# Permuted q, k and v rows, two-bank score tiles, a token MLP per pair, and transposes moved from TensorE to DMA in an attention + mixer kernel

## The chip, the core and the metric

The kernel runs on one core of one Trainium2 chip. The metric is device microseconds (us) of one execution. The four executions of the kernel before spread over 0.5% (465.88 to 467.99 us). The engines are named as in the profile: PE is TensorE's matmuls, PEld its weight loads (they overlap PE: in the kernel before 415.4 and 250.1 us of a span of 463.9), DVE is VectorE, ACT is ScalarE, POOL is GpSimd, SP is SyncE, which here only issues DMAs. PEclk is the clock that TensorE was granted, as a share of full speed. A run is called fast when it is at most 1.5% above the fastest of the same kernel beside it, else slow.

## The reference, cut to what matters

```python
# q, k, v: 8 batches x 12 heads x 448 rows x 64, float32
q_n = q / (norm(q) + 1e-6);  k_n = k / (norm(k) + 1e-6)
attn = softmax(q_n @ k_n.T / tau)            # 448 x 448 for each head
x = (attn @ v).transpose(0, 2, 1, 3).reshape(8, 448, 768)
h = relu(x.T @ w_tok1) @ w_tok2              # token MLP, 448 -> 256 -> 448
u = x + h.T
out = u + relu(u @ w_ch1) @ w_ch2            # channel MLP, 768 -> 1536 -> 768
```

Two heads are handled together as a *pair*: there are 48 pairs, numbered 0 to 47, six for each batch. q, k and v are loaded by the *half batch*, six heads or three pairs at a time: 672 KB each for q, k and v.

## The kernel before

For each pair GpSimd and VectorE normalise q and k; TensorE transposes them (eight 112x112 transposes); TensorE computes scores; ScalarE takes the exponential; TensorE multiplies with v ("PV"). While the pairs of batch b run, TensorE's free slots are filled with the MLPs of the batches before. Three parts matter here. First, a pair's scores use a single PSUM tile of four banks, so a score must wait for the exp before it:

```python
    ps2 = ctx.enter_context(tc.tile_pool(name="ps2", bufs=1, ...))
    def score(i, cg):                      # called twice a pair
        psS = ps2.tile([128, 2, 2, 512], FP32, ...)
        for j in range(2):
            for hh in range(2):
                nc.tensor.matmul(psS[:, hh, j, 0:S], ...)
        nc.scalar.activation(out=st["pt"][:, cg], in_=psS[0:SC, :, :, 0:S], func=AF.Exp, scale=inv_tau)
```

Second, q/k are transposed on TensorE, and VectorE copies the result out of PSUM:

```python
    def tpose(i):
        for a, src in enumerate((st["kn"], st["qn"])):
            for c in range(NCH):
                nc.tensor.transpose(pst[:, a, c, :], src[:, c], id16[:SC, :SC])
        nc.vector.tensor_copy(out=qk[:], in_=pst[:].rearrange("p a c s -> p a (c s)"))
```

Third, the residuals are added on TensorE by matmuls with an identity (four in token layer two, three in each output tile):

```python
        for i in range(3):
            nc.tensor.matmul(psF[:, 128 * i:128 * (i + 1)], rows(ut, 3 * dh + i), id16[:], start=False, stop=(i == 2))
        ...                                # [cut: VectorE / ScalarE copies to SBUF, stores]
```

## Time and profile before

| | before |
|---|---|
| median of 4 runs (465.88 to 467.99) | 467.04 us |
| span of the profiled run, mean granted clock | 463.9 us, 0.997 |
| PE busy | 415.4 us, 90% |
| bytes moved by DMA | 50.02 MB |
| eighth pair's (pair 7's) first score | 67.55 us |

From the page of the kernel before: the busy time of each engine, PE's busy tenths in 40 equal slices with the granted clock below them, and the chain of work that ended last, by engine.

```profile
PE 415.4 (90%) x4136; PEld 250.1 (54%) x4136; DVE 218.9 (47%) x442; ACT 232.1 (50%) x262; POOL 218.8 (47%) x220
...
PE   0505889999999999999999999999999999999995
...
PEclk9999999999999999999999999999999999999998
...
PE 84%; ACT 6%; DVE 4%; POOL 2%; issue 2%; DMA 1%; SPq 0%; ACTq 0%; POOLq 0%
```

PE is the bound: 90% busy, 84% of the chain. The page has its granted clock at 9 tenths or more in all slices but the last. No other engine is over half busy. So work taken off TensorE should shorten the run, as long as TensorE keeps its inputs.

From the timeline of the kernel before, around 33, 67 and 202 us (start, duration, engine, line, what; in brackets the idle time before it and what ended it):

```profile
33.81 0.93 PE L199 MATMUL psS_1_290<-qk_185 64*128 64x448 f16 x4 [10.95 <-ACT pt_251 L201]
...
67.55 0.56 PE L199 MATMUL psS_0_714<-qk_666 64*128 64x448 f16 x4 [1.14 <-ACT pt_630 L201]
...
201.68 0.55 PE L199 MATMUL psS_0_2815<-qk_2767 64*128 64x448 f16 x4 [1.14 <-ACT pt_2723 L201]
```

In the start, scores take 0.93 us for four matmuls and wait for others, once 11 us. Later they take 0.55, and now and then wait up to 1.14 us for the exp that still holds the only score tile.

### The profile page before, as it was taken

What the parts mean: (1) busy time and instruction counts of PE and PEld (TensorE: products, weight loads), DVE (VectorE), ACT (ScalarE), POOL (GpSimd) and SP (SyncE); (2) the same over time, 40 slices, a digit from 0 to 9 for tenths busy, and PEclk for the clock granted to TensorE, in tenths of its full rate; (3) what the DMA queues carried; (4) which work ended last, traced back from release to release, by engine and by line L of the source; (5) the groups of instructions that cost most, each with busy time, mean ns of one, the idle gap of its engine ahead of it and who ended that gap; (6) DMA issues with size and microseconds to landing.
All of it is one profiled execution on the core that took longest, in us unless ns stands there. A gap on an engine that the chain in (4) does not pass through costs nothing.

```text
span 463.9 us, 9519 instructions
## 1 busy us (share of the span) xinstructions
PE 415.4 (90%) x4136; PEld 250.1 (54%) x4136; DVE 218.9 (47%) x442; ACT 232.1 (50%) x262; POOL 218.8 (47%) x220
## 2 busy tenths in 40 slices
PE   0505889999999999999999999999999999999995
PEld 0203556556654566555655566556655666556563
DVE  2558659555564455445645445445735343224000
ACT  2324666775467544574457443674367534520410
POOL 4699698678374834374383725474472200000000
PEclk9999999999999999999999999999999999999998
DMA  9997999951485046721574065902100001000012
GB/s 205 237 235 175 223 204 229 209 120 32 125 188 119 1 129 154 167 47 37 134 192 102 1 165 117 206 9 78 52 35 1 35 35 56 15 34 35 34 54 83
DMA packets 72842, 50.02 MB, mean 108 GB/s; under 512 B 44449, under 2 KB 68449, under 8 KB 72801
## 3 DMA queue, kind: packets, MB, share of 16 engines
q1 hardware_dynamic: 69408, 44.05, 39.6%
q0 software_dynamic: 3392, 5.37, 6.3%
q8 instruction: 32, 0.52, 0.5%
q14 instruction: 10, 0.07, 0.1%
HBM read 43.78 MB, written 11.01 MB: 118 GB/s over the span
## 4 chain that ended last, share of the span: by engine, by line
PE 84%; ACT 6%; DVE 4%; POOL 2%; issue 2%; DMA 1%; SPq 0%; ACTq 0%; POOLq 0%
DMA qh_105<-in_q_dram 1%; DVE kn_324 L175 1%; DVE ssq_118 L157 1%; ACT pt_630 L201 1%; ACT pt_482 L201 1%; ACT pt_1042 L201 1%; DVE ssq_126 L157 0%; POOL sq_207 L152 0%; PE psF_2_1_5429 L279 0%; PE psF_2_0_5377 L279 0%; PE psF_1_1_5303 L279 0%; PE psF_0_0_5164 L279 0%; PE psF_2_1_4787 L279 0%; PE psF_2_0_4717 L279 0%; PE psF_1_1_4651 L279 0%
## 5 line engine op out<-in xcount | busy, mean ns | idle before, releaser
L260 PEld LDWEIGHTS <-wc1t 128*128 128x128 f16 x576 | 51.5, 97 | 52.0 <-issue 10.7
L279 PEld LDWEIGHTS <-gt_2_3862 128*128 128x128 f16 x168 | 15.3, 98 | 12.8 <-issue 2.6
L279 PEld LDWEIGHTS <-gt_1_2351 128*128 128x128 f16 x168 | 15.4, 98 | 12.5 <-issue 2.6
L279 PEld LDWEIGHTS <-gt_0_804 128*128 128x128 f16 x168 | 15.5, 98 | 11.4 <-issue 1.5
L279 PEld LDWEIGHTS <-gt_3_5342 128*128 128x128 f16 x168 | 15.9, 98 | 9.6
L228 PEld LDWEIGHTS <-w1t 128*128 128x128 f16 x128 | 10.9, 97 | 8.0 <-issue 2.6
L199 PE MATMUL psS_1_290<-qk_185 64*128 64x448 f16 x4 | 0.9, 557 | 11.0 <-ACT pt_251 L201 11.0
L183 PE MATMUL pst_145<-id_86,kn_143 112*128 112x112 f16 x4 | 0.6, 291 | 9.1 <-DVE kn_143 L175 9.1
L199 PEld LDWEIGHTS <-qk_185 64*128 64x128 f16 x8 | 0.5, 104 | 13.6 <-issue 12.9
L285 DVE COPY ost_0_6031<-psF_0_0_6032 128x384 f32<-128x384 f32 x1 | 0.6, 557 | 15.2 <-PE psF_0_0_6032 L282 15.2
L164 ACT ACTIVATE rn_119<-ssq_118,tiny 112x16 f32<-112x16 f32 x3 | 0.9, 307 | 12.1 <-DVE ssq_118 L157 12.1
L175 POOL TENSOR_TENSOR qn_5044<-qh_4311,rn_4315 112x512 f16<-112x512 f32 x1 | 1.0, 1041 | 10.3 <-DVE rn_4315 L167 10.3
L164 ACT ACTIVATE rn_109<-ssq_108,tiny 112x16 f32<-112x16 f32 x3 | 0.9, 304 | 8.6 <-DVE ssq_108 L157 8.6
L183 PEld LDWEIGHTS <-kn_143 112*128 112x128 f16 x4 | 0.3, 129 | 9.1 <-DVE kn_143 L175 9.1
L175 DVE TENSOR_TENSOR kn_324<-kh_116,rn_119 112x512 f16<-112x512 f32 x1 | 4.7, 4745 | 0.0
L282 PEld LDWEIGHTS <-ut_0_803 128*128 128x128 f16 x42 | 3.5, 98 | 1.8
L282 PEld LDWEIGHTS <-ut_1_2350 128*128 128x128 f16 x42 | 3.5, 98 | 1.8
L282 PEld LDWEIGHTS <-ut_2_3861 128*128 128x128 f16 x42 | 3.5, 98 | 1.8
L282 PEld LDWEIGHTS <-ut_3_5341 128*128 128x128 f16 x42 | 3.5, 98 | 1.8
L175 POOL TENSOR_TENSOR qn_3954<-qh_3191,rn_3195 112x512 f16<-112x512 f32 x1 | 1.0, 1042 | 7.3 <-PE psU_3_3986 L252 7.3
L199 PE MATMUL psS_0_400<-qk_365 64*128 64x448 f16 x4 | 0.9, 564 | 3.8 <-DVE qk_365 L185 3.8
L152 POOL TENSOR_TENSOR sq_2301<-qh_2033 112x512 f32<-112x512 f32 x1 | 1.0, 1039 | 6.9 <-DVE ssq_1701 L157 6.9
(1726 smaller groups left out, 1299.7 us busy)
## 6 DMA issues: line engine op xcount, KB each, us to landing
wc1t<-in_moe_w_ch_dram POOLq DMA_DIRECT2D x2, 1152.0 KB, 13.0
wc2t<-in_moe_w_ch_dram POOLq DMA_DIRECT2D x2, 1152.0 KB, 15.4
vs_107<-in_v_dram SPq DMA_DIRECT2D x1, 672.0 KB, 7.8
qh_115<-in_q_dram SPq DMA_DIRECT2D x1, 672.0 KB, 10.2
kh_116<-in_k_dram SPq DMA_DIRECT2D x1, 672.0 KB, 12.2
vs_117<-in_v_dram SPq DMA_DIRECT2D x1, 672.0 KB, 8.3
qh_123<-in_q_dram SPq DMA_DIRECT2D x1, 672.0 KB, 10.8
kh_124<-in_k_dram SPq DMA_DIRECT2D x1, 672.0 KB, 12.6
```

What stands on the lines that cost most here:

```text
L152: nc.gpsimd.tensor_mul(out=sq[:, a], in0=src, in1=src)
L157: nc.vector.tensor_reduce(out=half[i // HP]["ssq"][:, :, lo:lo + 2 * NCH], in_=pipe[i]["sq"][:], axis=AXX.X, op=ALU.add)
L164: nc.scalar.activation(out=rn, in_=ssq, func=AF.Ln, bias=tiny[:])
L175: eng.tensor_tensor(out=dst[:].rearrange("p c g e -> p g c e"), in0=src, in1=_bcast_free(rn, E), op=ALU.mult)
L183: nc.tensor.transpose(pst[:, a, c, :], src[:, c], id16[:SC, :SC])
L199: nc.tensor.matmul(psS[:, hh, j, 0:S], qk[hb:hb + 64, c * SC:c * SC + 128], qk[hb:hb + 64, S:2 * S], start=True, stop=True)
L201: nc.scalar.activation(out=st["pt"][:, cg], in_=psS[0:SC, :, :, 0:S], func=AF.Exp, scale=inv_tau)
L228: nc.tensor.matmul(psR[:], w1t[:, m, tt * 128:(tt + 1) * 128], x16[b][:, m, dh * DH:(dh + 1) * DH], start=(m == 0), stop=(m == 3))
L260: nc.tensor.matmul(psG[:], wc1t[:, dt, ct * 128:(ct + 1) * 128], ut[:, dt, span(b)], start=(dt == 0), stop=(dt == DT - 1))
L279: nc.tensor.matmul(psF[:], rows(gt, ct), wc2t[:, ct, dh * DH:(dh + 1) * DH], start=(ct == 0), stop=False)
L282: nc.tensor.matmul(psF[:, 128 * i:128 * (i + 1)], rows(ut, 3 * dh + i), id16[:], start=False, stop=(i == 2))
L285: nc.vector.tensor_copy(out=o[:, 0:DH], in_=psF[:])
```

## The change

The intent is to take about 27 us off TensorE and to fill the start. q's rows are permuted as k's and v's already were (row `4p + c` in place of `112c + p`), so each partition reads 1 KB runs of all three, and the token MLP's weights and the output's rows follow that order. The score tile becomes two tiles of two banks. The token MLP runs for each pair by itself, which gives u by rows; VectorE adds both residuals. u of pairs 6 to 47, and q/k of pairs 12 to 47, are transposed by DMA (`DMA_TRANSPOSE`) on SP's queue, where the q, k, v loads and the output stores are issued too. The diff, cut to its core:

```diff
-    outp = ctx.enter_context(tc.tile_pool(name="outp", bufs=3))
-    ps2 = ...(tc.tile_pool(name="ps2", bufs=1, space=bass.MemoryType.PSUM))
+    outp = ctx.enter_context(tc.tile_pool(name="outp", bufs=2))
+    ps2 = ...(tc.tile_pool(name="ps2", bufs=2, space=bass.MemoryType.PSUM))
+    DMA_T0 = 12
...
+    def tpose_dma(i):
+        st["qk"] = att.tile([128, 2, NCH, SC], FP16, name=f"qk_{i}", tag="qk")
+        nc.sync.dma_start_transpose(out=st["qk"][:]..., in_=st["kq"][:]...)
...
+    def tok2(i, pe=False):
+        ...                                        # eight 128x128 matmuls into psU
+        nc.vector.tensor_tensor(out=u, in0=psU[:], in1=st["x"][:], op=ALU.add)
+        if pe: return
+        nc.sync.dma_start_transpose(out=ut[b][:, pj], in_=u.rearrange("p m d -> p (m d)"))
...
-        for i in range(3):
-            nc.tensor.matmul(psF[:, 128 * i:128 * (i + 1)], rows(ut, 3 * dh + i), id16[:], ...)
+            nc.vector.tensor_tensor(out=o..., in0=psF..., in1=u16[bb]..., op=ALU.add)
...
+            # in the loop over pairs, pairs 0 to 5:
+                done = [[], [], [], [0, 1], [2, 3], [4]][i]
+                for t in done:
+                    tok1(t)
+                    tok2(t, pe=True)
+                    upose(t)
+            # pairs 6 and on:
+            if i % HP == 1 and (i + 8) // HP < NHALF:
+                load_half((i + 8) // HP)           # q, k and v, 2 MB, every third pair
+            if DMA_T0 <= i + 1 < NP_ALL:
+                tpose_dma(i + 1)                   # for the next pair
+            ...                                    # [cut: scores, PV, MLP pieces of pair i]
```

## The prediction

> **What bounds the kernel now.** TensorE. On the page PE is busy 90% of the 463.9 us span; the chain that ended last is 84% PE. From the timeline I took each matmul group's slot (start to next start, unstalled): score 4 matmuls 0.48 us, PV 16 in 0.51, four transposes 0.20 (8 and a gap: 0.49), token layer one 4x384 0.65, token layer two 0.37 plus its four identity matmuls 0.19, channel layer one 6x448 1.13, channel layer two 12x384 1.95 plus three identity matmuls 0.16. Times their counts this is 388 us. The rest: 9 us before the first matmul, 38 us of stalls and slow early matmuls up to 60 us (pair 7's score starts at 67.5 us), 23 us of later stalls (mostly score waiting for exp to free its single 4-bank tile, 1.14 us each), 5 us after the last matmul.

> **TensorE work removed and added.** Transposes of pairs 12-47: -36x8 at 0.05 = -14.4 us. Output identity matmuls: -8.8. Token layer two with identities 26.9 -> 48x8x0.056 = 21.5 (-5.4). Token layer one 20.8 -> 21.5 (+0.7). PE transposes of u, six pairs: +1.3. Sum -26.6: 388 -> 362 us. All on the critical path.

> **Start.** The stretches show DMA saturated until about 92 us at 205-215 GB/s while 256 B q rows load, 250-300 when only 1 KB runs do. Permuted q has 1 KB runs; ACT and POOL norm work is reordered, which held exp of pair 1 until 32 us (waits: ACT on ssq_118, on POOL sq_207). Exp becomes 4x about 0.93 instead of 2x1.66 us a pair (estimate). Six pairs at about 5.5 us (POOL, ACT and DVE each 4-5 us) from about 10 us, also doing five pairs' token MLP: pair 7 starts at about 47 us instead of 67.5. wc1t must land by then: 11 MB at 250 GB/s = 44 us, tight.

> **After that.** 362 less 23 us done by then = 339 us of PE slots. Two score tiles remove most 1.14 us waits; 8 us stalls stay. DVE gains adds but loses copies; ACT loses 13.4 us of output copies, gains about 19 us of exp overhead; both stay under 70%.

> **DMA transposes.** 36 of 229 KB, 42 of 131 KB, on SP's queue. None is in this trace. [...]against one pair (7.4 us) of lead. But every third pair three 672 KB loads are queued directly ahead (k lands 1.9 us after q): the transpose lands about 10 us after issue and score waits 1-3 us, ten times or so. Output stores with two buffers also queue behind loads. Together 12 us.

> **Sum.** 47 + 339 + 8 + 12 + 5 = 411; tuning may hide part: **408 us, 80% range 394 to 428**. Faster by over 2%: 0.96, same 0.03, slower 0.01.

> **What would show it.** Slots as above; pair 7's score start near 47 us; no score waits on ACT over 1 us in steady state; waits of score on DMA qk in every third pair; final 5 us unchanged.

> **What would make it wrong.** DMA transposes far slower than copies (over 7 us each stalls every pair: 450 or more); small token matmuls limited by weight loads; wc1t late; DVE blocked by output buffers; or transposes entirely hidden and a start under 42 us (near 393).

The sum: 47 + 339 + 8 + 12 + 5 = 411, and 3 less for tuning, 408. The landing of about 10 us behind three loads fits the prediction's own 205 to 215 GB/s: three loads of 672 KB are 2.06 MB, which is 9.6 to 10.1 us at that rate.

## The result, and the profile after

Ratios here and below are the mean time of one kernel's fast runs over that of the other's fast runs of the same rounds, so not quite the ratio of the medians that are quoted.

| | before | after |
|---|---|---|
| median | 467.04 us | 522.53 us (518.23 to 525.93, 4 runs) |
| ratio, 95% interval | | 1.1186 (1.1123 to 1.1249): slower |
| span, mean granted clock | 463.9, 0.997 | 522.0, 0.902 |
| PE busy | 415.4 us (90%) | 416.1 us (80%) |
| bytes moved by DMA | 50.02 MB | 63.87 MB |
| pair 7's first score | 67.55 us | 75.66 us |

The result is correct. The predicted 408 us was far off, and on the wrong side.

The same lines of the page, after (and the chain by line):

```profile
PE 416.1 (80%) x4056; PEld 249.7 (48%) x4056; DVE 208.0 (40%) x436; ACT 233.8 (45%) x362; POOL 213.9 (41%) x222
...
PE   1575687969695897949879496984949999999996
...
PEclk9995689898988797988979699896988999999999
...
PE 63%; DMA 20%; POOL 7%; issue 4%; DVE 3%; ACT 2%; SPq 0%; DVEq 0%; POOLq 0%
PE psG L324 20%; PE psF L339 19%; DMA qk<-kq 19%; PE psO L275 10%; PE psS L259 8%; POOL sq L199 3%; PE psU L302 3%; PE psR L288 3%; POOL kq L230 3%; DMA kh<-in_k_dram 1%; DVE ssq L208 1%; ACT pt L261 1%; POOL vt L184 1%; PE pst L244 0%; DVE ost L343 0%
```

Three things are to be seen. PE's row, all 9s before, has a dip to 4 or so at regular distances, until about 400 us. The granted clock has dips at the same places. And the transposes of q/k by DMA are now 19% of the chain. PE's busy time did not fall (416.1 us against 415.4), although it has less work (4056 matmuls against 4136): it does it more slowly, at a mean granted clock of 0.902 against 0.997.

The waits of PE's scores after (total us, times, longest):

```profile
PE psS L259 <- DMA qk<-kq: 62.5, 10, 9.3
...
PE psS L259 <- ACT pt L261: 3.3, 5, 1.5
```

Ten waits, 62.5 us. The waits for the exp, which the two-bank tiles were to remove, are indeed nearly gone. One of the ten, from the timeline of the kernel after, with what SP issued ahead of it (SPq lines are issues):

```profile
249.72 0.55 PE L259 MATMUL psS<-qk 64*128 64x448 f16 x4
...
250.20 1.19 PE L275 MATMUL psO<-vt,pt 112*128 112x65 f16 x32
...
250.56 1.54 SPq L308 DMA_TRANSPOSE ut<-u  x1
...
252.19 0.53 SPq L97 DMA_DIRECT2D qh<-in_q_dram  x1
...
252.77 0.51 SPq L102 DMA_DIRECT2D kh<-in_k_dram  x1
...
253.38 0.47 SPq L114 DMA_DIRECT2D vs<-in_v_dram  x1
...
253.94 4.92 SPq L251 DMA_TRANSPOSE qk<-kq  x1
...
264.33 0.93 PE L259 MATMUL psS<-qk 64*128 64x448 f16 x4 [5.60 <-DMA qk<-kq]
265.19 1.94 PE L275 MATMUL psO<-vt,pt 112*128 112x65 f16 x32
266.94 3.26 PE L339 MATMUL psF<-wc2t,gt 128*128 128x384 f16 x12
270.13 0.55 PE L259 MATMUL psS<-qk 64*128 64x448 f16 x4
```

The pair that begins at 249.72 needs about 9 us of PE work. SP first issues the transpose of u (it had to wait for VectorE's sum), then three loads, then at 253.94 the transpose of the next pair. This lands only at about 264.3, 10.3 us after it was issued, and 14.6 us after the pair began; PE sits idle for 5.6 us. Then PE works at half speed for a while: the scores take 0.93 us in place of 0.55, PV 1.94 in place of 1.19; the granted clock is 0.50 from 262.5 to 269.3 us. Issuing the transpose took SP 4.92 us here; in the kernel after the issue of a q/k transpose took 1.25 us in the median and 5.69 at most, one of u 1.20 in the median, and SP issued nothing else meanwhile.

The issue-to-landing times of the q/k transposes (229 KB each) in the kernel after, from the view of that tile:

```profile
DMA to landing us min/median/max: 2.9/4.0/10.9
```

The same for the transposes of u (131 KB each):

```profile
DMA to landing us min/median/max: 2.4/2.7/7.5
```

So the transpose itself lands in 2.9 us (q/k) or 2.4 us (u) at best. It is the one behind the loads that takes 10 us. The chain of waits, in order of time, has such pieces at 111.77 (6.67 us), 133.10, 161.32, 193.66, 223.78, 253.94, 285.78, 316.04, 349.02 and 379.03 (8.95 to 10.89 us): every third pair, just where a half batch is loaded. After 400 us, when all is loaded, there are none.

The start got later too. The timeline of PE in the kernel after, between 43 and 50 us, and its first score of pair 7:

```profile
43.09 1.01 PE L302 MATMUL psU<-rt,w2t 128*128 128x128 f16 x8 [5.47 <-DVE rt L291]
44.89 0.61 PE L314 MATMUL psT<-id,u 128*128 128x128 f16 x4 [0.79 <-DVE u L305]
45.29 1.06 PE L288 MATMUL psR<-x,w1t 128*128 128x128 f16 x8
46.86 1.01 PE L302 MATMUL psU<-rt,w2t 128*128 128x128 f16 x8 [0.52 <-DVE rt L291]
48.66 0.61 PE L314 MATMUL psT<-id,u 128*128 128x128 f16 x4 [0.79 <-DVE u L305]
49.20 0.93 PE L259 MATMUL psS<-qk 64*128 64x448 f16 x4
...
75.66 0.55 PE L259 MATMUL psS<-qk 64*128 64x448 f16 x4
```

The token MLPs of the first pairs are issued in a row, each step waiting for the VectorE step before it, with no score in between; ScalarE meanwhile has nothing to exponentiate (its exp at 49.86 us was idle 11.96 us before).

### The profile page after: what moved, and what is told of

It reads as the page before. It is cut to its first block, busy times and chain, and to the rows that moved or that the text cites. A ratio compares the mean times of both kernels' runs of the same rounds, so it can differ in the third digit from the quotient of the medians.

```text
span 522.0 us, 9727 instructions
## 1 busy us (share of the span) xinstructions
PE 416.1 (80%) x4056; PEld 249.7 (48%) x4056; DVE 208.0 (40%) x436; ACT 233.8 (45%) x362; POOL 213.9 (41%) x222
## 2 busy tenths in 40 slices
DMA packets 97243, 63.87 MB, mean 122 GB/s; under 512 B 58176, under 2 KB 92736, under 8 KB 97200
## 4 chain that ended last, share of the span: by engine, by line
PE 63%; DMA 20%; POOL 7%; issue 4%; DVE 3%; ACT 2%; SPq 0%; DVEq 0%; POOLq 0%
PE psG L324 20%; PE psF L339 19%; DMA qk<-kq 19%; PE psO L275 10%; PE psS L259 8%; POOL sq L199 3%; PE psU L302 3%; PE psR L288 3%; POOL kq L230 3%; DMA kh<-in_k_dram 1%; DVE ssq L208 1%; ACT pt L261 1%; POOL vt L184 1%; PE pst L244 0%; DVE ost L343 0%
## 5 line engine op out<-in xcount | busy, mean ns | idle before, releaser
L261 ACT ACTIVATE pt<-psS 112x896 f16<-112x896 f32 x192 | 165.5, 914 | 185.4 <-PE psS L259 185.3
L324 PE MATMUL psG<-ut,wc1t 128*128 128x448 f16 x576 | 128.4, 365 | 0.0
L339 PE MATMUL psF<-wc2t,gt 128*128 128x384 f16 x672 | 122.5, 337 | 0.0
L259 PE MATMUL psS<-qk 64*128 64x448 f16 x384 | 62.8, 403 | 69.1 <-DMA qk<-kq 62.5
L339 PEld LDWEIGHTS <-gt 128*128 128x128 f16 x672 | 65.2, 101 | 47.3 <-issue 11.3
L327 ACT ACTIVATE gt<-psG 128x448 f16<-128x448 f32 x96 | 52.3, 545 | 68.1 <-PE psG L324 68.1
L324 PEld LDWEIGHTS <-wc1t 128*128 128x128 f16 x576 | 52.7, 100 | 50.9 <-issue 13.8
L275 PEld LDWEIGHTS <-pt 112*128 112x128 f16 x1536 | 62.2, 108 | 23.7 <-issue 19.1
L275 PE MATMUL psO<-vt,pt 112*128 112x65 f16 x1536 | 69.3, 209 | 0.0
L208 DVE TENSOR_REDUCE ssq<-sq 112x16 f32<-112x1024 f32 (+1 forms) x49 | 57.9, 1186 | 14.0 <-POOL sq L199 9.5
L259 PEld LDWEIGHTS <-qk 64*128 64x128 f16 x384 | 12.5, 97 | 93.1 <-DMA qk<-kq 64.4
L230 POOL TENSOR_TENSOR kq<-qh,rn 112x512 f16<-112x512 f32 x48 | 50.0, 1042 | 3.8 <-DVE rn L222 3.8
L302 PE MATMUL psU<-rt,w2t 128*128 128x128 f16 x384 | 30.5, 224 | 10.9 <-DVE rt L291 10.8
## 6 DMA issues: line engine op xcount, KB each, us to landing
vs<-in_v_dram SPq DMA_DIRECT2D x16, 672.0 KB, 10.2
```

The costliest lines, as they stand in the source:

```text
L208: nc.vector.tensor_reduce(out=half[i // HP]["ssq"][:, a0:a1, lo:lo + 2 * NCH], in_=pipe[i]["sq"][:, a0:a1], axis=AXX.X, op=ALU.add)
L230: (eng or nc.gpsimd).tensor_tensor(out=st["kq"][:, a].rearrange("p c g e -> p g c e"), in0=side(i, a), in1=_bcast_free(rn, E), op=ALU.mult)
L259: nc.tensor.matmul(psS[:, hh, 0:S], qk[hb:hb + 64, c * SC:c * SC + 128], qk[hb:hb + 64, S:2 * S], start=True, stop=True)
L261: nc.scalar.activation(out=pts[i % 2][:, 2 * S * c:2 * S * (c + 1)].rearrange("p (h s) -> p h s", h=2), in_=psS[0:SC, :, 0:S], func=AF.Exp ...
L275: nc.tensor.matmul(psO[:, m, 0:E + 1], pts[i % 2][:, at:at + 128], vt[:, g, c, 0:E + 1], start=(c == 0), stop=(c == NCH - 1))
L302: nc.tensor.matmul(psU[:, m], w2t[:, tt, lo:lo + 128], st["rt"][:, tt], start=(tt == 0), stop=(tt == TT - 1))
```

## The experiments

Fifteen kernels ran, all variants of one of the two; e7, e9, e12, e15 and e16 beat both by over 2%, e16 by most. Five of them are one execution each, of unknown state (e1, e3, e4, e5, e11), so their times are less sure than the others', which come from several rounds, all fast but one run of e17. The rounds ran on different chips; the kernel before ran beside each. Each is set beside runs of the kernel before on the same chip (medians 466.13 to 467.66 us where there were rounds; 466.35 in the single look of e1, e3, e4 and e5).

The theories: **A**, a q/k transpose waits behind the three loads in SP's queue, and its lead of one pair is too short. **B**, the order in the queue hardly matters, as a transpose beside loads is slow wherever they are queued. **D**, the start is late because of the serial token chains. **E**, the start is bound by the rate of the loads. **F** and **G** differ in what the two-bank score tiles alone are worth. A2 and B2 are A and B for what was left later. One correction: when I wrote the expectations I took the score at 70.32 us in the kernel after for pair 7's. It is pair 6's; pair 7's is at 75.66.

### e11: is it the loads?

The kernel after, with the loads from half batch 5 on removed and old data used. Its output is wrong, which doesn't matter for the time.

```diff
     def new_half(n):
+        if n > 4:
+            half[n] = dict(half[4], ssq=..., rn=...)   # old q, k, v
+            return
...
     def load_half(n):
         new_half(n)
+        if n > 4:
+            return
```

> The changed kernel with the suspected cause taken away: from half 5 on nothing is loaded, q, k and v of half 4 are used again (wrong result on purpose); order of all transposes as in the changed kernel. Theory A: the ten waits (62.5 us) vanish to under 5 us, the slow-clock stretches behind them too: 435 us (428 to 446). Rival B (the transposes are slow by themselves, or the u transpose ahead of them is what holds them): waits over 20 us remain, time over 455.

Measured: 439.72 us, span 437.7, clock 0.967. The wait of the scores for q/k transposes, total, times and longest, in this kernel:

```profile
PE psS L265 <- DMA qk<-kq: 0.5, 2, 0.3
```

Landing of q/k transposes fell to 2.9/2.9/4.6 us (minimum, median, maximum), of u to 2.4/2.4/4.5. So with nothing else in the queue the transposes are harmless, and the loads cost the kernel about 83 us (522.53 less 439.72). Shown: it is the loads beside the transposes, not the transposes as such.

### e1: the transpose ahead of the loads

```diff
-            if i % HP == 1 and (i + 8) // HP < NHALF:
-                load_half((i + 8) // HP)
             ...
             if DMA_T0 <= i + 1 < NP_ALL:
                 tpose_dma(i + 1)
+            if i % HP == 1 and (i + 8) // HP < NHALF:
+                load_half((i + 8) // HP)
```

> Edit: in each pair's program the q/k DMA transpose of the next pair is issued before the three 672 KB loads of a later half, not behind them. Theory A (the transpose waits behind the loads in the one SP queue): the ten waits of score on DMA qk (62.5 us) fall to under 8 us in all, the slow-clock matmuls that follow each wait go too (granted clock from 0.90 to 0.95 or more), time about 435 us (425 to 448). Rival B (a DMA transpose beside loads is slow by itself, whatever the order): the waits stay or move to other pairs, time over 500. Rival C (what the kernel lost lies in smaller token matmuls and the start, the waits only fill slack): waits go but time stays over 480.

Measured: 478.85 us, between the ranges of A (425 to 448) and B (over 500); waits for q/k 22.3 us in 9, the longest 4.4. Order matters: 44 us were won by swapping two statements. But the waits do not vanish, as the transposes of the following pair now stand behind the same loads, and VectorE now waits 15.4 us for output buffers.

### e3: the loads on another queue

```diff
-        nc.sync.dma_start(out=half[n]["q"]...
+        (nc.gpsimd if n > 4 else nc.sync).dma_start(out=half[n]["q"]...   # k and v likewise
```

> Edit: order as in the changed kernel, but q/k/v loads from half 5 on are issued on the POOL queue, transposes stay on SP. Theory A: the transpose has no load ahead of it in its own queue; [...]it lands in 4 to 7 us and the waits of score on DMA qk fall below 15 us in all; about 445 us (430 to 465). Rival B (contention for the DMA engines, not order in the queue): landing stays near 10 us in the load pairs, waits stay over 40 us, time over 490.

Measured: 498.31 us; waits for q/k 42.5 us in 9, the longest 9.6; longest landing 13.8 us for q/k, 14.5 for u. This is what B expected (over 490 us, waits over 40), and not what A did. Taking the loads out of SP's queue helped less than e1 did. A 229 KB transpose took up to 13.8 us although no load was ahead of it in its own queue, against 2.9 us in the median where no late loads ran at all (e11). By what means the loads of one queue delay the transposes of another was not shown. So B has a part in it: here a separate queue was no cure.

### e4: q/k on TensorE

```diff
-    DMA_T0 = 12
+    DMA_T0 = 48
```

> Edit: all q/k transposes on TensorE (none by DMA), u still by DMA. Theory A: waits of about 62 us and some 25 us of slow matmuls after them go, 36 pairs of transposes come back at about 14 us: about 448 us (438 to 462). Rival C: the time stays over 480, because the loss is elsewhere.

Measured: 455.31 us, clock 0.979, no waits for q/k. This hit. The rest of the change is worth some 11 us against the kernel before (466.35 beside it), and the DMA transposes of q/k as written cost 67 us.

### e5: u on TensorE, q/k by DMA

```diff
-            tok2(i - 1, pe=(i - 1 < NPAIR))
+            tok2(i - 1, pe=True)
...
                 score(i, 1)
+                if i > NPAIR + 1:
+                    upose(i - 2)       # four transposes on TensorE, behind the next scores
```

> Edit: u transposed on TensorE for all pairs (four matmuls, about 0.22 us, placed after the next pair's first scores), q/k still by DMA behind the loads. Theory A: the u transposes are not what is waited for; TensorE gains about 9 us, each of the ten waits may get 1 to 2 us shorter because one transpose less is issued ahead: 505 to 530 us, the waits on DMA qk stay over 45 us. Rival B' (any transposes in the queue slow the whole): the waits fall by more than half and the time below 480.

Measured: 481.78 us, where 505 to 530 was expected: a miss. The order of loads and q/k transposes is as in the kernel after, and the longest landing is even 12.6 us, yet the waits fell to 11.5 us in 3. What changed is when they are issued. In the kernel after, SP waits for u before it issues what stands behind it: its own waits ahead of the transposes of u that ended with one kind of VectorE step (the reciprocal next to u's sum) are 142.7 us in 25. The line for this from SP's own waits in the kernel after:

```profile
SPq L308 <- DVE rec L278: 142.7, 25, 11.5
```

Without them in SP's program, loads and transposes are issued almost a pair earlier. So the delay has two parts: when SP comes to issue the transpose, and how long it takes to land. Neither harms alone: e11 has 143.0 us of the same waits of SP, and no q/k wait over 0.3 us. The rival B' had expected this fall of the waits (and under 480 us). e5 by itself does not exclude it; but the longest landing did not get shorter without u's transposes, and in e11 all transposes stayed in the queue and did no harm.

### e2: the transposes two pairs ahead

```diff
-            if DMA_T0 <= i + 1 < NP_ALL:
-                tpose_dma(i + 1)
...
             for t in sc_now:
                 if t < NP_ALL:
                     scaled(t)                     # t = i + 2
+                    if t >= DMA_T0:
+                        tpose_dma(t)
```

> Edit: the q/k DMA transpose of pair i+2 is issued in pair i right after its scaling on POOL, ahead of the u transpose of that pair, instead of at the start of pair i+1 behind the u transpose and the loads. Theory A' (SP issues in order; a q/k transpose is held first by the u transpose's wait for VectorE, then by three loads, together about 14 us after the pair starts, against 9 us of lead): with 14 to 16 us of lead no wait of score on DMA qk over 2 us, under 6 us in all; no slow-clock stretch after 110 us; the time is that of e4 (455) less about 14 us of transposes on TensorE: 441 us (433 to 450). Rival B (transposes are slow beside loads, landing over 14 us): waits over 20 us remain, time over 460.

Measured: 457.37 us (454.98 to 460.77), ratio 0.9792 (0.973 to 0.9855); waits for q/k 12.5 us in 5. Most of the loss is gone with the lead alone, but 441 us was missed. The transposes behind loads still land up to 11.0 us after issue.

### e6: the start interleaved, and e7: both

The token steps of pairs 0 to 5 are placed between the scores of later pairs in place of a row, and two sums of VectorE are moved later:

```diff
+        early = [([], [], []), ([], [], []), ([], [], [t1(0)]),
+                 ([t2(0)], [up(0), t1(1)], [t2(1), t1(2)]),
+                 ([up(1), t2(2)], [up(2)], [t1(3)]),
+                 ([t2(3)], [up(3)], [t1(4)])]     # tok1, tok2, upose by pair and place
...
                 score(i, 1)
+                for f in early[i][0]: f()
...
-                for t in done:
-                    tok1(t); tok2(t, pe=True); upose(t)
+                for f in early[i][2]: f()
```

> Edit: start only, transposes as in the changed kernel. The token layers of pairs 0 to 5, which run as chains matmul, VectorE, matmul, VectorE, transpose with nothing between, are spread between scores and PVs of the following pairs, and two sums that hold VectorE for POOL come after them. Theory D (the start is bound by these chains, 24 us of serial time between 37 and 76 us, not by the rate of the loads): the seventh pair's second-next score (pair 7) starts at 55 to 62 us instead of 70, whole 505 to 515 us, later waits on DMA qk unchanged. Rival E (start bound by arrival of weights or of q/k/v): pair 7 still starts at 68 us or later, 518 to 526 us.

e6 measured 506.1 us (502.58 to 508.32), ratio 1.0819 (1.0765 to 1.0873): 16 us less than after, in the expected range. The q/k waits stay (59.6 us in 10).

> Both edits together (two pairs of lead, interleaved start). If both theories hold and are independent: 441 less 10 to 15 us = about 428 us (418 to 440), beating both kernels. If the start's gain only moves a wait: the time of e2 within 1%.

e7 is e2 and e6 together: 440.64 us (439.99 to 441.55), ratio 0.9427 (0.94 to 0.9454), just over the expected range of 418 to 440, and the first version faster than both kernels by over 2%. Pair 7's first score is at 60.34 us. 10.6 us of waits for q/k are left. D is shown for the edit as a whole: the start's order costs 16 to 17 us, and this adds to the other gains. What the two moved sums have in it was not tried apart.

### e8: the kernel before with q in 1 KB runs

```diff
-        nc.sync.dma_start(out=half[n]["q"]... "p g c e -> p (g c) e"), in_=q[...]"g (c p) e -> p (g c) e", p=SC))
+        nc.sync.dma_start(out=half[n]["q"]... "p g c e -> p g (c e)"), in_=q[...]"g (p c) e -> p g (c e)", c=NCH))
```

(The output rows then come out permuted: wrong.)

> The kernel before with one part of the change: q loaded in 1 KB runs (rows permuted, so its output rows come in permuted order: wrong on purpose). Theory D: the start is not bound by the loads' rate; the time stays within 1% of before (462 to 468 us). Rival E (my prediction's reading, 205 GB/s with 256 B runs against 250 to 300 with 1 KB): the start shortens by 5 us or more, 452 to 461 us.

Measured: 467.9 us, ratio 1.0004 (0.9975 to 1.0032). The mean DMA rate of the first 60 us is 212 GB/s, against 216 in the kernel before. What falls is the prediction's reading that longer runs raise the rate: those of q are worth nothing here, neither in rate nor in time. That no part of the start is bound by the loads is not shown: in e16 the chain that ended last begins with one load of k, from 3.93 to 23.03 us.

### e10: the kernel before with two score tiles of two banks

```diff
-    ps2 = ...bufs=1...
+    ps2 = ...bufs=2...
-        psS = ps2.tile([128, 2, 2, 512], FP32, ...)      # one exp for four matmuls
+        for j in range(2):
+            psS = ps2.tile([128, 2, 512], FP32, ...)     # one exp for two
```

> The kernel before with one part of the change alone: score tiles of two banks, two in flight, an exp each, instead of one of four banks (result unchanged). Theory F: most of the waits of score on exp after 60 us (up to 23 us) go, ACT's added fixed cost of about 19 us lies off the critical path: 450 us (444 to 458). Rival G: the waits only move to PV or to the psum tiles, time 461 to 469.

Measured: 461.1 us (460.71 to 461.64), ratio 0.9882 (0.986 to 0.9904). The step is worth 1.2%, at G's edge and less than F's. The long waits for the exp did go: after 60 us there are 4.5 us in 14, none over 0.4 us.

### e9 and e12: the loads behind the transposes, all three together

e9 is e7 with the three loads issued after `tpose_dma(i + 2)`:

```diff
-            if i % HP == 1 and (i + 8) // HP < NHALF:
-                load_half((i + 8) // HP)
...
                     if t >= DMA_T0:
                         tpose_dma(t)
+            if i % HP == 1 and (i + 8) // HP < NHALF:
+                load_half((i + 8) // HP)
```

> e7 (two pairs of lead, interleaved start) plus: the three loads of a half are issued behind the q/k transpose of that pair instead of at the pair's start. In e2 and e7 the waits that are left (13 us in five) belong to transposes issued right behind loads and landing 11 us later. Theory A': those go, no wait of score on DMA qk over 1 us; 430 us (424 to 436). Rival: what is left is the transposes' own slowness beside loads, which now run beside the next pair's transpose: waits of 2 to 4 us stay, time within 1% of 440.6.

Measured: 447.3 us (446.78 to 449.13), ratio 0.9593 (0.9566 to 0.962): slower than e7. From its waits:

```profile
DVE ost L343 <- DMA out_dram<-ost: 25.5, 4, 8.1
PE psU L302 <- DVE rt L291: 17.6, 6, 5.4
PE psS L259 <- DMA qk<-kq: 5.6, 4, 1.7
```

The q/k waits fell from 10.6 to 5.6 us. Now the output stores stand behind the loads: VectorE waits 25.5 us for one of the two output buffers, and as its steps go in order, the relu of the token MLP comes late and PE waits for that. The cost moved from one user of the queue to another. A third output buffer would be the direct test; it does not fit in SBUF (the build of e9 with it stops: the pool would take 9 KB of each partition, 6.25 KB are left), so that stays untried.

e12 is e9 with VectorE's sums and norms of pairs 6 to 8, and what hangs on them, moved behind the token steps of pair 4's turn:

```diff
-                    sums(6); sums(7); squares(8); sums(8); norms(6, 9); ...
+                    squares(8)
...
                 for f in early[i][2]: f()
+                if i == 4:
+                    sums(6); sums(7); sums(8); norms(6, 9); scaled(6); cast_v(2); load_half(4)
```

> e9 plus: in the start, the three sums and the norms of pairs 6 to 8, which hold VectorE for 4 us before the token layer's eviction of pair 3, come after it. Expected 2 to 5 us under e9 (the wait of 3.9 us at 44 us and the slow clock behind it go, but the first scaling for pair 6 starts 1 us later). Rival: unchanged, since POOL's scaling for pair 6 waits for these norms.

Measured: 447.22 us (446.73 to 449.01), the same as e9's 447.3. The wait of token layer two moved to the transpose of u, where one of 4.2 us came up. No gain.

### e15 and e16: the burst, and whether DMA transposes pay

e16 is e7 with one load a pair, behind that pair's transpose, in place of three every third pair. The bytes, the queue and all else are the same. e9 (447.3 us) has the three loads at that same place, so from e9 to e16 only the spreading differs.

```diff
-            if i % HP == 1 and (i + 8) // HP < NHALF:
-                load_half((i + 8) // HP)
...
                     if t >= DMA_T0:
                         tpose_dma(t)
+            n = (i + 8 - (i - 1) % HP) // HP
+            if 5 <= n < NHALF:
+                if i % HP == 1:
+                    new_half(n)
+                    load_q(n)
+                elif i % HP == 2:
+                    load_k(n)
+                else:
+                    load_v(n)
```

> The combined version, with the q, k and v loads of a half issued one per pair, each behind that pair's q/k transpose, in place of three together every third pair. Theory A2 (the burst is the cause: a transpose or a store waits for the 2 MB issued just ahead of it, and would wait only a third as long behind 0.67 MB): waits on the q/k transposes and on the output stores both fall under 5 us in sum, longest landing of a transpose under 7 us, time 428 us (420 to 436). Rival B2 (what is left is sharing of the engines by bytes, or the start and TensorE's own work, and order in the queue no longer matters): 438 to 444 us, with the q/k waits only spread thinner.

> The changed kernel with the start interleaved and all q/k transposes on TensorE (u still by DMA). Theory: the two gains add, 455.3 - 16 = 439 us (433 to 445), with no waits on q/k transposes; so transposing late q/k by DMA, whose TensorE share was about 36 x 0.4 us = 14 us, has gained nothing in the combined version of 440.6 us, and gains only if the loads are spread (e16 faster than this by over 5 us). Rival: TensorE transposes cost more in the loop than their slots say (VectorE copies in the chain): 447 or more.

e15 (e4 and e6 together) measured 436.01 us (435.47 to 438.17), ratio 0.9326 (0.9308 to 0.9343): the two gains add. e16 measured **422.36 us** (421.47 to 423.34), ratio **0.904** (0.9019 to 0.9061), correct, clock 0.991. From the page of e16:

```profile
PE 385.4 (91%) x4056; PEld 233.9 (55%) x4056; DVE 205.0 (49%) x436; ACT 233.9 (55%) x362; POOL 214.4 (51%) x222
...
PE   1449588898999999999999999999999999999995
...
PEclk9999899899999999999999999999999999999999
```

From the list of its waits, the one of VectorE for an output buffer:

```profile
DVE ost L343 <- DMA out_dram<-ost: 4.9, 3, 1.9
```

No wait of a score for a q/k transpose is left on the list, VectorE's wait for stores fell from 25.5 (e9) to 4.9 us, and q/k transposes land in 2.9/3.3/5.7 us. Those of u still take up to 9.4 us, where under 7 was expected of every transpose. Its timeline at about the time shown of the kernel after:

```profile
249.62 1.36 SPq L308 DMA_TRANSPOSE ut<-u  x1
251.07 1.25 SPq L251 DMA_TRANSPOSE qk<-kq  x1
...
252.38 0.57 SPq L102 DMA_DIRECT2D kh<-in_k_dram  x1
...
257.39 0.55 PE L259 MATMUL psS<-qk 64*128 64x448 f16 x4
257.87 1.19 PE L275 MATMUL psO<-vt,pt 112*128 112x65 f16 x32
```

The transpose of the pair after next is issued at 251.07, ahead of the one load, and issuing it costs SP 1.25 us in place of 4.92. Neither the scores nor PV are slowed.

Against e15, e16 gains 13.7 us (436.01 less 422.36). The prediction had the 36x8 transposes at 14.4 us of PE time. e16 also spreads the loads, which e15 does not; but PE is busy 400.3 us in the profiled run of e15 and 385.4 in that of e16, and idle 36.1 us in both, so the gain is work taken off PE. So here DMA transposes of q/k pay in full once no score waits for them; in e7, at 440.64, they had paid nothing.

### e17: spreading alone

The kernel after with only the loads spread; each still ahead of the next pair's transpose, which has still one pair of lead.

```diff
-            if i % HP == 1 and (i + 8) // HP < NHALF:
-                load_half((i + 8) // HP)
+            n = (i + 8 - (i - 1) % HP) // HP      # q, k, v of half n at i, i + 1, i + 2, as in e16
```

> The changed kernel with one edit: the q, k and v loads of a half are issued one a pair instead of three together every third pair, at the same place of the pair, ahead of the next pair's transpose; the lead of one pair, the start and all else as in the changed kernel. Theory A2 (the burst is the cause): each transpose stands behind 0.67 MB in place of 2 MB, lands 5 to 7 us after issue in place of 10 to 11, inside the lead of about 9 us less the 4 us in which it is issued: waits on q/k transposes under 20 us in sum, none over 2.5, time 452 us (442 to 465). Rival (the short lead is the cause, and now every pair waits in place of each third): the waits stay at 40 us or more in many small ones of 1 to 2 us, time 480 to 505.

Measured: 472.94 us (471.53 to 478.82, the highest a slow run; the profiled one, 477.53, is the slowest of the four fast ones), ratio 1.0121 (1.0101 to 1.0141), between the two expected ranges. The wait of its scores for q/k:

```profile
PE psS L259 <- DMA qk<-kq: 25.6, 13, 3.4
```

The landing of its q/k transposes, from the view of that tile:

```profile
DMA to landing us min/median/max: 2.9/5.6/7.4
```

The landing is as A2 had it (5 to 7 us); the waits are more and somewhat longer than it allowed (under 20 us, none over 2.5). Spreading alone wins about 50 of the 100 us between after and e16, but the lead of one pair is too short even for one load. Lead alone (e2) gave 65 us, lead and start (e7) 82, all three (e16) 100. The gains of lead and spreading overlap and cannot be added.

This run also shows the clock. Three of its waits and what came after them, from its timeline:

```profile
163.38 0.55 PE L259 MATMUL psS<-qk 64*128 64x448 f16 x4 [2.19 <-DMA qk<-kq]
163.87 1.72 PE L275 MATMUL psO<-vt,pt 112*128 112x65 f16 x32
165.40 2.38 PE L324 MATMUL psG<-ut,wc1t 128*128 128x448 f16 x6
...
199.07 0.55 PE L259 MATMUL psS<-qk 64*128 64x448 f16 x4 [1.24 <-DMA qk<-kq]
...
225.60 0.92 PE L259 MATMUL psS<-qk 64*128 64x448 f16 x4 [3.02 <-DMA qk<-kq]
```

After the wait of 1.24 us all runs on at full speed. After 3.02 us the scores take 0.92 in place of 0.55. After 2.19 us the scores still take 0.55, but the PV behind them takes 1.72 in place of 1.19, and six matmuls of channel layer one 2.38 in place of 1.31: the granted clock is 0.50 from about 164.2 to 167.6. Of this run's seven waits between 1.71 and 2.31 us, five were followed by such a stretch. All ten waits of the kernel after (3.86 us and more) were.

## Why the prediction was wrong

The stretches before and after pair 7's first score, of the kernel after and of e16, show where the difference went, as both have the same 4056 matmuls on TensorE. The columns are the stretch, its length, the busy time of PE, PEld, DVE, ACT and POOL with their instructions, the granted clock, the share of DMA and GB/s. First the kernel after:

```profile
0.00:75.66 75.66, 42.42 (x433) 27.96 (x434) 35.71 (x76) 32.88 (x50) 46.62 (x60) 0.84 0.94 212
75.66:522.00 446.34, 373.72 (x3626) 221.69 (x3624) 172.26 (x360) 200.96 (x312) 167.31 (x162) 0.91 0.50 107
```

The same two stretches of e16:

```profile
0.00:60.35 60.35, 34.16 (x432) 22.95 (x434) 34.58 (x76) 32.97 (x50) 41.59 (x55) 0.97 1.00 216
60.35:421.50 361.15, 351.26 (x3626) 210.91 (x3624) 170.40 (x360) 200.95 (x312) 172.83 (x168) 0.99 0.67 141
```

From pair 7 on, the same 3626 matmuls take 446.3 us in the one and 361.2 in the other. Of these 85.2 us, PE's busy time accounts for 373.7 - 351.3 = 22.5 us (half speed after waits), and its idle time (72.6 against 9.9 us) for 62.7. Before pair 7 another 15.3 us are lost. e16's pair 7, from its timeline:

```profile
60.35 0.55 PE L259 MATMUL psS<-qk 64*128 64x448 f16 x4
```

Term by term, the sum of the prediction was 47 + 339 + 8 + 12 + 5 = 411:

- **"Together 12 us" for DMA transposes and stores: this step failed.** The mechanism was there word for word: "every third pair three 672 KB loads are queued directly ahead", "lands about 10 us after issue", about ten times. All of that was measured (ten waits; 8.95 to 10.9 us for all but the first). What was mis-sized is the wait, put at 1 to 3 us and measured at 6.25 us on average, 62.5 in sum. The prediction set the landing of 10 us against a lead of a whole pair (7.4 us). But the transpose is issued only 4.2 us after the pair began, behind a wait of SP for VectorE and four issues; so of a pair of 9 us not 9 but about 5 us of lead are left. e5 and e2 show this part (earlier issue, same landing or longer: waits of 11.5 and 12.5 us), e17, e1 and e16 the queue's part.
- **The sum had no term for the clock.** About each of the ten waits the granted clock was 0.50 for 3.4 to 10.2 us, partly while TensorE still waited. From pair 7 on PE's busy time is 22.5 us longer by the stretches above. The prediction had itself seen slow matmuls in the start of the kernel before, and did not ask when they would come back.
- **"pair 7 starts at about 47 us": failed.** It came at 75.66. The step was "six pairs at about 5.5 us [...] also doing five pairs' token MLP". The token layers were issued as serial chains between PE and VectorE, 49.2 less 45.3 or some 4 us for one pair, during which no score ran. e6 and e7 show it: interleaved, pair 7 starts at 60.3 us, and the time falls by 16 to 17 us. The remaining 13 us above 47 were not settled: in e16 PE is busy 34.2 of the first 60.4 us with DMA busy all through (a share of 1.00, 216 GB/s), its chain begins with 19.1 us of one load of k, and in e8 longer runs of q did not lift the rate of the kernel before (212 GB/s against 216 in the first 60 us).
- **"250-300 when only 1 KB runs do. Permuted q has 1 KB runs": failed as a reason for a faster start.** e8: ratio 1.0004, and no higher DMA rate (212 GB/s against 216). What the 250 to 300 GB/s of some stretches came with was not looked for; in stretches of 4 us the kernel before reaches 264 at most in its first 92 us.
- **PE's work, "388 -> 362 us": about right; "339 + 8 + 12 + 5" from pair 7 on: near, in part by luck.** PE's busy time falls by 30.0 us from the kernel before to e16 (415.4 to 385.4), predicted 26.6. In e16 the stretch from pair 7 takes 361.2 us, where the prediction's terms sum to 364; but 12 of these were for waits on DMA, and e16 has no q/k wait left. Without them the sum is 352, 9 us too low. Of the small token matmuls layer one ran as costed (0.45 us for eight, start to next start, estimated at 8x0.056), layer two took 0.54; the rest of the 9 us was not traced. e16 against e15 gives 13.7 us for the q/k transposes, predicted 14.4.
- **What a DMA transpose takes to land** depends on what is beside it. With no late loads it is 2.9 us in the median (229 KB) and 2.4 (131 KB, both e11); for comparison, a store of 240 KB landed in 2.6 us in the median (after). Right behind 2 MB of loads in the same queue it is 8.95 to 10.9 us (after, all but the first of the ten), with 0.67 MB ahead in most pairs 5.6 us in the median (e17), and beside loads in another queue up to 13.8 us (e3).
- **"No score waits on ACT over 1 us in steady state": about right**, 3.3 us in 5 waits; e10 prices the two-bank tiles at 5 to 6 us of the kernel before. An exp of a two-bank tile took 0.914 us in the mean (192 of them, after), estimated at about 0.93, against 1.66 for one of four banks (96, before): some 16 us more in sum, where about 19 was expected. The "23 us of later stalls (mostly score waiting for exp" was too high: 8.9 us of such waits are in that trace after 60 us.
- **"What would make it wrong"** named transposes that take over 7 us, but as slow hardware that "stalls every pair". It was every third pair, and by the program's order.
- **Output buffers blocking VectorE** was named as a risk. In the kernel after it did not show, in e1 (15.4 us) and e9 (25.5 us) it did.

## What to carry to other kernels

When work moves from a busy engine to DMA, count its latency from when the issuing engine gets to it, behind everything in program order on that engine (here 4.2 us after the pair began), to when it lands behind everything in the queue (10.3 us later), and set this against the lead that is left then, not against the time of a stage. Bulk loads that were harmless in the kernel before became here the latency of the small DMAs behind them that the critical engine waited for (8.95 to 10.9 us for nine of ten, in place of 2.9 in e11): issue them in small pieces behind the urgent ones, and issue the urgent ones two stages ahead; here this, with a start whose token steps are interleaved, turned 11.9% slower into 9.6% faster with the same matmuls on TensorE. Long idle times on TensorE cost more here than they lasted, about a third more (22.5 us on 62.7), since the granted clock was 0.50 about them; five of seven waits between 1.71 and 2.31 us did this too (e17).
